# A linear-attention kernel with a token mixer: another written order, constants built with fewer instructions, and the last two output tiles computed in halves

## The chip, the core and the metric

The kernel runs on one core of a Trainium2 chip. The core has a matrix engine (PE in the profile, with its weight loads as PEld), three engines that work on 128 partitions at once (DVE, ACT, POOL), and a queue engine (SP) that here only starts transfers. The metric is the time of one execution on the device in microseconds (us); lower is better.

## The reference

For each of 4 batches and 8 heads, attention with a decay of `lam` per token runs over blocks of 64 tokens of 64 features: inside a block with a masked product, between blocks through a state. The eight heads side by side are then the input `x` of a mixer over tokens.

```python
for b in range(nb):                                   # 12 blocks of 64 tokens
    intra = einsum('bhic,bhjc->bhij', qb, kb) * Dmask[None]     # lam ** (i - j), lower triangle
    intra = einsum('bhij,bhjd->bhid', intra, vb)
    inter = einsum('bhid,bhde->bhie', qb * lam_pow[None], kv_state)
    out[:, :, sl] = intra + inter
    kv_state = lam_block * kv_state + einsum('bhsd,bhse->bhde', kb * rev_pow, vb)
...
x = out as [4, 768, 512]
W_tok = (x @ w_q) @ (x @ w_k).T / 8                   # [768, 768] per batch
result = maximum(W_tok @ x, 0) @ w_out                # [4, 768, 512], float32
```

## The kernel before

The kernel works on 16 pairs of heads, n = 0 to 15, four pairs to a batch, and on chunks of 128 tokens, six to a sequence. Decay is taken out of the blocks: q is multiplied by lam^t (the tiles `dq`) and v by lam^-t (the tile `DvI`), so that the mask is a plain triangle. The operands of the matrix engine are bf16, sums are f32.

All instructions are issued in an order written out by hand, the string `ORDER`. A word is a piece, its index, the PSUM bank it uses (`@`), and the engine that does it (`:a` ACT, `:v` DVE, `:p` POOL). Each engine takes its own instructions in that order, and waits where an operand or a bank is not ready. The pieces:

- `q`, `k`, `v`, `wq`, `wk`, `wo`: loads with a cast from f32 to bf16, all issued on POOL's queue (lines 113, 117, 121, 127, 132, 140). Eight semaphores take turns, so that a load is issued only when the one eight places earlier has landed.
- `sv`: v times `DvI`, in place, on DVE or POOL (line 239).
- `Aq`, `Ak`: transposes of q and k on PE (251, 260); `eq`, `ek`: their copies out of PSUM, `eq` with the factor `dq` (266, 234).
- `S0`, `S1`: scores of the first and the last three chunks (277). `M0`, `M1`: DVE multiplies them with the mask on the way out of PSUM (291). `Mc` and `Mm` do this in two steps: ACT copies the scores out (306), DVE multiplies in place (310). This form exists for the first half only.
- `P`: states, the running sums of k times v (319). For n below `WHOLE` = 6 every chunk adds to all later ones; from there on the first two chunks add to two places only, and `G` (copy of the states, 328) adds the missing part on DVE in three instructions (335 to 337).
- `I`, `V`: the two products that make the attention output (347, 359); `ex`: its copy to `xnat`. `F`, `ef`: its transpose with the permutation `order` (382) and the copy to `xT`.
- `Q` (in parts `Qp`), `K`, `Y`, `m` with their copies: the mixer's products for a batch (404, 414, 430, 455, 479, 490). `O`, `eo`: a 128x512 output tile, its copy out of PSUM and its store on SP's queue (508, 519). Twelve tiles `osb` hold outputs.
- `Z`: matmuls of zeros (528), 512 columns each, which keep PE at work; nine stand at the start.
- `hold`: a small transfer on SP's queue that waits for k of pair 14, so that no store starts earlier.

Tokens are permuted inside a chunk: q is loaded in pairs of rows, and `order` brings the attention output to the same sequence. `ident` and `order` are built on DVE from a ramp `ET` and the partition number `row` (lines 157 to 203); `blank` is the tile of zeros.

Of the kernel before, what the change touches and what calls it, by code (L numbers as in the profile page):

```python
# [9 lines left out]
BF16 = mybir.dt.bfloat16  # L10
F32 = mybir.dt.float32
ALU = mybir.AluOpType
ACT = mybir.ActivationFunctionType

B, H, S, D = 4, 8, 768, 64
CH = 128
NCH = S // CH
HD = H * D
DHY = 64
NP = H // 2  # L20
HALF = 3 * CH
N = B * NP
WHOLE = 6
R = (slice(0, 64), slice(64, 128))
# [5 lines left out]
q.2 k.2 v.2 q.3 k.3 v.3 wq.0 wk.0 q.4 k.4 v.4 wo.0 q.5 k.5 v.5 q.6 k.6 v.6 q.7 k.7 v.7 sv.4:p q.8  # L30
k.8 v.8 sv.5:p q.9 k.9 v.9 q.10 k.10 v.10 sv.7:p q.11 k.11 v.11 q.12 k.12 v.12 sv.9:p q.13 k.13
v.13 sv.10:p q.14 k.14 v.14 sv.11:p q.15 k.15 v.15 sv.12:p sv.13:p sv.14:p hold.14 Aq.0@0 dq.2
eq.0@0 dq.3 Z.5@7 Ak.0@0 dq.1 ek.0@0:v Z.3@7 S1.0@0 sv.0:v S0.0@2 Mc.0@2 M1.0@0 Z.3@7 P.0@4 Aq.1@5
G.0@4:a Mm.0:v Z.1@7 I.0@0 eq.1@5 Ak.1@4 V.0@0 ek.1@4:v ex.0@0:a S0.1@4 sv.1:v S1.1@2 Mc.1@4 Z.1@7
F.0@0 M1.1@2 P.1@1 ef.0@0:a Aq.2@4 Mm.1:v G.1@1:a eq.2@4 Z.1@7 Ak.2@0 I.1@2 ek.2@0:v V.1@2 S1.2@0
sv.2:v ex.1@2:a S0.2@4 Mc.2@4 M1.2@0 Z.3@7 P.2@2 Aq.3@3 G.2@2:a Mm.2:v F.1@4 eq.3@3 Ak.3@2
ef.1@4:v I.2@0 V.2@0 ek.3@2:v ex.2@0:a sv.3:v Z.1@7 S0.3@2 S1.3@4 cw.0:a M1.3@4 Mc.3@2 Z.2@7 P.3@0
Qp.0.0@1 F.2@6 G.3@0:a Mm.3:v Qp.0.1@1 ef.2@6:a I.3@4 V.3@4 Qp.1.0@0 ex.3@4:a Aq.4@6 Ak.4@7 eq.4@6
F.3@4 ek.4@7:a Qp.1.1@0 Qp.0.2@1 eg.3.0@4:v Qp.1.2@0 eg.3.1@4:v Qp.0.3@1 eQ.0.0@1:v Qp.1.3@0
S1.4@4 eQ.0.1@0:a Kh.0.0@1 M1.4@4 ek2.0.0@1:a Kh.0.1@0 S0.4@6 ek2.0.1@0:a M0.4@6 Y.0@0 YA.0@0:a  # L40
YB.0@0:v Aq.5@1 YC.0@0:a m.0.1@6@7 eq.5@1 m.0.0@4@5 eh.0.1.0@6:a eh.0.0.0@4:v eh.0.0.1@5:a Ak.5@1
eh.0.1.1@7:a m.0.2@4@6 ek.5@1:v m.0.3@5@0 eh.0.2.1@6:a eh.0.3.1@0:v S0.5@2 eh.0.3.0@5:a S1.5@6
eh.0.2.0@4:v P.4@0 O.0.5@5 G.4@0:v M1.5@6 I.4@0 eo.0.5@5:a V.4@0 M0.5@2 Aq.6@4 ex.4@0:a Ak.6@5
eq.6@4 O.0.4@6 ek.6@5:a sv.6:v S1.6@4 S0.6@0 M1.6@4 F.4@7 O.0.3@2 ef.4@7:a M0.6@0 P.5@3 eo.0.3@2:a
Ak.7@7 G.5@3:v Aq.7@0 ek.7@7:a P.6@2 eq.7@0 I.5@4 V.5@4 G.6@2:v S0.7@0 ex.5@4:a eo.0.4@6:v Aq.8@7
M0.7@0 I.6@2 S1.7@4 O.0.0@6 eq.8@7 M1.7@4 V.6@2 eo.0.0@6:a O.0.2@7 ex.6@2:a sv.8:v P.7@6
eo.0.2@7:a Ak.8@2 G.7@6:v P.8@3 ek.8@2:a F.5@7 G.8@3:v Aq.9@6 ef.5@7:a Ak.9@2 eq.9@6 S1.8@4
ek.9@2:a S0.8@0 I.7@6 M1.8@4 V.7@6 F.6@2 ex.7@6:a M0.8@0 O.0.1@3 ef.6@2:v F.7@6 eo.0.1@3:a Aq.10@7
ef.7@6:v S0.9@2 eq.10@7 S1.9@0 Ak.10@6 M1.9@0 Q.1.0@7 ek.10@6:a M0.9@2 Q.1.1@4 eQ.1.0@7:a I.8@6
eQ.1.1@4:a S1.10@0 P.9@5 M1.10@0 K.1@4 V.8@6 eK.1@4:a G.9@5:v Aq.11@2 ex.8@6:a Y.1@4 eq.11@2  # L50
Ak.11@5 YA.1@4:a YB.1@4:v S0.10@2 ek.11@5:v YC.1@4:a m.1.0@6 M0.10@2 em.1.0@6:a m.1.1@0 Aq.12@5
P.10@4 em.1.1@0:a eq.12@5 m.1.3@2 I.9@6 G.10@4:v em.1.3@2:a V.9@6 m.1.2@0 ex.9@6:v I.10@4
em.1.2@0:a F.8@2 V.10@4 ef.8@2:v S0.11@0 ex.10@4:a S1.11@6 M0.11@0 O.1.1@2 M1.11@6 F.9@3
eo.1.1@2:a O.1.0@0 ef.9@3:a Ak.12@2 eo.1.0@0:a P.11@3 ek.12@2:v Ak.13@1 Aq.13@0 G.11@3:v ek.13@1:a
S1.12@6 S0.12@4 eq.13@0 I.11@2 V.11@2 M0.12@4 O.1.4@0 ex.11@2:a M1.12@6 F.10@1 eo.1.4@0:a F.11@2
ef.10@1:a S0.13@6 ef.11@2:v S1.13@4 Ak.14@0 M1.13@4 P.13@1 ek.14@0:a Aq.14@2 G.13@1:v Q.2.0@3
eq.14@2 Q.2.1@0 eQ.2.0@3:a M0.13@6 S1.14@2 eQ.2.1@0:a I.13@4 O.1.5@1 M1.14@2 V.13@4 sv.15:v
eo.1.5@1:a P.14@0 ex.13@4:a Aq.15@2 G.14@0:v K.2@1 Ak.15@3 eK.2@1:a P.12@4 eq.15@2 P.15@0
ek.15@3:a Y.2@1 G.12@4:v G.15@0:v S0.14@4 YB.2@1:a S0.15@2 I.12@6 YA.2@1:a M0.14@4 V.12@6 YC.2@1:a
O.1.2@0 ex.12@6:a M0.15@2 S1.15@4 eo.1.2@0:a I.14@6 m.2.1@2 M1.15@4 F.12@1 em.2.1@2:a V.14@6  # L60
ef.12@1:a I.15@4 ex.14@6:v m.2.2@2 V.15@4 em.2.2@2:a F.13@0 ex.15@4:v F.14@1 ef.13@0:a m.2.0@2
m.2.3@6 ef.14@1:v F.15@4 em.2.0@2:a O.1.3@0 ef.15@4:v em.2.3@6:a Q.3.0@1 eo.1.3@0:a Q.3.1@6
eQ.3.0@1:a O.2.0@0 eQ.3.1@6:v K.3@1 eo.2.0@0:v O.2.4@6 eK.3@1:a Y.3@7 eo.2.4@6:a O.2.3@6 YA.3@7:v
YB.3@7:v YC.3@7:v m.3.1@0 eo.2.3@6:a O.2.2@4 em.3.1@0:a m.3.0@6 eo.2.2@4:a m.3.2@2 m.3.3@0
em.3.0@6:v O.2.5@5 em.3.2@2:a em.3.3@0:a O.2.1@4 eo.2.5@5:v O.3.0@0 eo.2.1@4:a O.3.2@1 eo.3.0@0:v
O.3.4@4 eo.3.2@1:a O.3.3@5 eo.3.4@4:v O.3.1@1 eo.3.3@5:a O.3.5@0 eo.3.1@1:a eo.3.5@0:a
# [4 lines left out]
def kernel(  # L71
# [11 lines left out]
    nc = tc.nc  # L83
    mm = nc.tensor.matmul
# [54 lines left out]
    def load_wo(_):  # L139
# [17 lines left out]
    blank = consts.tile([128, HD], BF16, name="blank")  # L157
# [3 lines left out]
    nc.vector.memset(step[:, 0:1], 1.0)  # L161
    nc.vector.memset(step[:, 64:65], -125.0)
    one = consts.tile([128, 1], F32, name="one")
    nc.vector.memset(one, 1.0)

    ET = consts.tile([128, S], F32, name="ET")
    nc.vector.tensor_tensor_scan(
        out=ET[:, 0:CH], data0=step, data1=step, initial=0.0, op0=ALU.add, op1=ALU.bypass
# [17 lines left out]
    token = consts.tile([128, 1], F32, name="token")  # L186
    nc.vector.tensor_tensor(out=token, in0=row, in1=row, op=ALU.add)
    for r in range(2):
        nc.vector.tensor_tensor(
            out=token[R[r], :], in0=token[R[r], :],  # L190
            in1=ET[R[r], (0, CH - 1)[r] : (1, CH)[r]], op=ALU.subtract,
        )

    order = consts.tile([128, 128], BF16, name="order")
    nc.vector.tensor_tensor(
        out=order.rearrange("e (p r) -> e p r", r=2), in0=natural,
        in1=token.unsqueeze(2).to_broadcast([128, 64, 2]), op=ALU.is_equal,
    )
    nc.vector.tensor_tensor(out=row, in0=row, in1=one, op=ALU.subtract)
    E6 = consts.tile([128, NCH], F32, name="E6")  # L200
    nc.vector.tensor_tensor(
        out=E6, in0=ET[:, ::CH], in1=row.to_broadcast([128, NCH]), op=ALU.add
# [10 lines left out]
    def make_dq(kk):  # L213
        nc.scalar.activation(out=Dq[kk], in_=ET, func=ACT.Exp, scale=lncol[:, kk : kk + 1])
# [18 lines left out]
    def copy(eng, to, of):  # L233
        return (nc.scalar.copy if eng == "a" else nc.vector.tensor_copy)(out=to, in_=of)  # L234
# [65 lines left out]
    def whole(n):  # L300
        return n < WHOLE


    def drawn(n, o):
        pr[n, 0] = tsb.tile([128, 2, HALF], BF16, tag="pr0", name="pr")
        nc.scalar.copy(out=pr[n, 0], in_=PS[:, o : o + 2, 0:HALF])

    def masked_late(n, eng):
        of = pr[n, 0].rearrange("j l (c i) -> j l c i", c=3)
        (nc.gpsimd if eng == "p" else nc.vector).tensor_tensor(  # L310
            out=of, in0=of, in1=mask2, op=ALU.mult
        )

    def states(n, o):
        to = PS[:, o, 0 : (NCH - 1) * D].rearrange("e (c f) -> e c f", c=NCH - 1)
        for c in range(NCH - 1):
            end = 2 if c < 2 and not whole(n) else NCH - 1
            for hl in range(2):
                mm(  # L319
                    to[R[hl], c:end, :],  # L320
                    fk[n][:, hl, c, :],
                    vn[n][:, hl, c, :].unsqueeze(1).to_broadcast([128, end - c, D]),
                    start=(c == 0),
                    stop=(c == NCH - 2),
                    skip_group_check=True,
                )

    def summed(n, o, eng):
        gs[n] = tsb.tile([128, NCH - 1, D], BF16, tag="gs", name="gs")
        of = PS[:, o, 0 : (NCH - 1) * D].rearrange("e (c f) -> e c f", c=NCH - 1)  # L330
        if whole(n):
            copy(eng, gs[n], of)
            return
        two = small.tile([128, 1, D], F32, tag="two", name="two")
        nc.vector.tensor_copy(out=two, in_=of[:, 1:2, :])
        nc.vector.tensor_copy(out=gs[n][:, 0:2, :], in_=of[:, 0:2, :])
        nc.vector.tensor_tensor(
            out=gs[n][:, 2:, :],
            in0=of[:, 2:, :],
            in1=two.to_broadcast([128, NCH - 3, D]),  # L340
            op=ALU.add,
        )
# [177 lines left out]

    held = consts.tile([1, D], BF16, name="held")
# [3 lines left out]

    def zeros(count, o):
        for _ in range(count):
            mm(PS[:, o, :], blank[:, 0:128], blank, start=True, stop=True)  # L528

    zeros(WARM, 7)  # L530
    make_dq(0)
    make_dv(0)
    pieces = dict(
        q=load_q, k=load_k, v=load_v, wq=load_wq, wk=load_wk, cw=copy_wq, wo=load_wo, hold=hold, dq=make_dq, dv=make_dv,
        sv=scale_v, Aq=turn_q, Ak=turn_k, eq=turned_q, ek=turned_k, S0=scores(0), S1=scores(1),
        M0=masked(0), M1=masked(1), Mc=drawn, Mm=masked_late, P=states, G=summed, I=inter, V=values, ex=attended, F=flip,
        ef=flipped, eg=flipped_half, Q=mix_q, eQ=mixed_q, K=mix_k, eK=mixed_k, Kh=mix_k_half, ek2=mixed_k_half, Y=mix_y, YA=mixed_y, YB=crossed_y(0), YC=crossed_y(1), Qp=mix_q_part, m=mix_m,
        em=mixed_m, eh=mixed_m_half, O=mix_o, eo=mixed_o, Z=zeros,
# [37 lines left out]
```

## Time and profile before

| | us |
|---|---|
| five runs | 98.55, 98.88, 99.70, 99.88, 99.95; median 99.7 |
| the profiled execution | 99.93 |
| its span, first to last instruction | 98.2 |
| mean granted clock | 0.995 |

Where the engines spend the span, in 40 slices of 2.46 us (a digit is the busy share in tenths):

```profile
PE   5999898599988999999799899999999999999930
DVE  5738892994789999998798599699999845544200
ACT  5576385258649367478457496776589992493440
POOL 5999996799669999999999999980000000000000
DMA  0999999999999999999999999999950202545782
```

The costliest group of each engine (instructions, busy time, mean of one; then idle time before them and who ended it):

```profile
L291 DVE TENSOR_TENSOR pr<-ps,mask 128x768 bf16<-128x768 f32 x28 | 25.9, 950 | 0.8 <-PE ps L277 0.7
L508 PE MATMUL ps<-wo,rmT 128*128 128x512 bf16 x86 | 22.7, 380 | 0.6 <-issue 0.2
L117 POOL DMA_DIRECT2D fk<-in_k_dram x16 | 16.7, 1047 | 1.5 <-DMA wo<-in_moe_w_out_dram 1.3
L234 ACT COPY osb<-ps 128x512 f32<-128x512 f32 x19 | 11.2, 588 | 10.0 <-PE ps L508 8.9
L239 POOL TENSOR_TENSOR fv<-fv,DvI 128x768 bf16<-128x768 bf16 x9 | 13.4, 1511 | 0.0
```

Line 234 is a helper's: all plain copies stand there, told apart by their tiles. A POOL instruction of a load is the making of its descriptors; the transfer itself follows and takes several us to land. Matmuls are pipelined, so the mean of one (380 ns for 512 columns) is longer than their spacing (32 of them take 7.03 us at the end, 0.22 each).

### The profile page before, as it was taken

To read this page: it belongs to the slowest core of one execution; us is meant where nothing else is said; L and a number is where in the kernel's file an instruction comes from. 1 tells how busy PE (TensorE), PEld (TensorE's weight loads), DVE (VectorE), ACT (ScalarE), POOL (GpSimd) and SP (SyncE) were. 2 spreads that over 40 slices of the span, in tenths; PEclk is the share of its full clock that TensorE was granted. 3 is DMA by queue.
4 is the path that set the end of the run, shared out by engine and by line. 5 is a ranking of instruction groups with operands and counts; after the bars stand their busy time and mean duration, and the time that the engine had idled before them with its cause. 6 is when DMAs were issued, how large, how long until landed. Compare 5 with 4: busy or idle time off the path is not lost.

```text
span 98.2 us, 3411 instructions
## 1 busy us (share of the span) xinstructions
PE 88.0 (90%) x1455; PEld 56.4 (57%) x1469; DVE 72.0 (73%) x140; ACT 61.5 (63%) x101; POOL 61.5 (63%) x65
## 2 busy tenths in 40 slices
PE   5999898599988999999799899999999999999930
PEld 1345675467564666767566586777696754534400
DVE  5738892994789999998798599699999845544200
ACT  5576385258649367478457496776589992493440
POOL 5999996799669999999999999980000000000000
PEclk9999999999999999999999999999999999999997
DMA  0999999999999999999999999999950202545782
GB/s 1 97 144 154 163 158 168 158 163 192 184 166 160 166 162 165 165 162 165 168 162 164 166 165 160 168 212 393 391 210 9 107 7 107 214 156 216 285 309 102
DMA packets 67438, 16.60 MB, mean 169 GB/s; under 512 B 63840, under 2 KB 64352, under 8 KB 67424
## 3 DMA queue, kind: packets, MB, share of 16 engines
q0 software_dynamic: 63792, 10.10, 139.3%
q1 hardware_dynamic: 3632, 6.30, 17.0%
q8 instruction: 11, 0.18, 0.7%
q14 instruction: 3, 0.02, 0.1%
HBM read 20.19 MB, written 6.29 MB: 270 GB/s over the span
## 4 chain that ended last, share of the span: by engine, by line
PE 66%; DMA 8%; POOL 8%; DVE 7%; issue 4%; ACT 3%; POOLq 0%; ACTq 0%
PE ps L508 21%; DMA fv<-in_v_dram 8%; PE ps L359 6%; PE ps L277 6%; PE ps L382 5%; PE ps L260 5%; PE ps L319 4%; PE ps L404 4%; PE ps L251 4%; PE ps L455 3%; POOL fk L117 3%; PE ps L347 3%; POOL fq L113 3%; PE ps L479 2%; POOL fv L121 2%
## 5 line engine op out<-in xcount | busy, mean ns | idle before, releaser
L291 DVE TENSOR_TENSOR pr<-ps,mask 128x768 bf16<-128x768 f32 x28 | 25.9, 950 | 0.8 <-PE ps L277 0.7
L508 PE MATMUL ps<-wo,rmT 128*128 128x512 bf16 x86 | 22.7, 380 | 0.6 <-issue 0.2
L117 POOL DMA_DIRECT2D fk<-in_k_dram x16 | 16.7, 1047 | 1.5 <-DMA wo<-in_moe_w_out_dram 1.3
L121 POOL DMA_DIRECT2D fv<-in_v_dram x16 | 16.7, 1042 | 1.6 <-DMA fv<-in_v_dram 1.2
L234 ACT COPY osb<-ps 128x512 f32<-128x512 f32 x19 | 11.2, 588 | 10.0 <-PE ps L508 8.9
L113 POOL DMA_DIRECT2D fq<-in_q_dram x16 | 14.1, 882 | 1.1 <-POOLq L560 0.8
L234 ACT CAST xnat<-ps 128x768 bf16<-128x768 f32 x13 | 10.4, 799 | 6.6 <-PE ps L359 6.3
L239 POOL TENSOR_TENSOR fv<-fv,DvI 128x768 bf16<-128x768 bf16 x9 | 13.4, 1511 | 0.0
L508 PEld LDWEIGHTS <-rmT 128*128 128x128 bf16 x96 | 8.3, 98 | 8.6 <-issue 0.7
L490 ACT ACTIVATE rmT<-ps 128x768 bf16<-128x768 f32 (+1 forms) x16 | 10.6, 722 | 0.2
L266 DVE TENSOR_TENSOR qT<-ps,dq 128x768 bf16<-128x768 bf16 x16 | 8.8, 553 | 2.2 <-PE ps L251 2.0
L528 PE MATMUL ps<-blank 128*128 128x512 bf16 x25 | 8.6, 471 | 1.5 <-DVE blank L158 1.2
L277 PE MATMUL ps<-qT,kT 64*128 64x128 bf16 x192 | 9.0, 218 | 0.6 <-DVE kT L234 0.5
L234 ACT COPY kT<-ps 128x768 bf16<-128x768 bf16 x9 | 7.2, 799 | 2.9 <-PE ps L260 2.4
L319 PE MATMUL ps<-fv,fk 128*64 128x128 bf16 (+4 forms) x160 | 7.8, 229 | 1.3 <-DVE fv L239 1.3
L359 PE MATMUL ps<-fv,pr 128*128 128x64 bf16 x192 | 8.5, 194 | 0.5 <-issue 0.5
L239 DVE TENSOR_TENSOR fv<-fv,DvI 128x768 bf16<-128x768 bf16 x7 | 7.1, 1010 | 2.0 <-DMA fv<-in_v_dram 2.0
L260 PE MATMUL ps<-ident,fk 128*64 128x128 bf16 x192 | 8.3, 221 | 0.2
L251 PE MATMUL ps<-ident,fq 128*64 128x128 bf16 x192 | 8.3, 221 | 0.1
L319 PEld LDWEIGHTS <-fk 128*64 128x64 bf16 x160 | 6.0, 110 | 4.0 <-DVE fv L239 2.2
L382 PE MATMUL ps<-order,xnat 128*128 128x128 bf16 x96 | 7.8, 220 | 0.2 <-ACT xnat L234 0.2
L277 PEld LDWEIGHTS <-kT 64*128 64x128 bf16 x192 | 5.6, 94 | 4.1 <-DVE kT L234 1.5
(68 smaller groups left out, 130.2 us busy)
## 6 DMA issues: line engine op xcount, KB each, us to landing
out_dram<-osb SPq DMA_DIRECT2D x24, 256.0 KB, 2.0
fq<-in_q_dram POOLq DMA_DIRECT2D x16, 192.0 KB, 7.6
fk<-in_k_dram POOLq DMA_DIRECT2D x16, 192.0 KB, 8.1
fv<-in_v_dram POOLq DMA_DIRECT2D x16, 192.0 KB, 8.1
wo<-in_moe_w_out_dram POOLq DMA_DIRECT2D x1, 512.0 KB, 8.7
wqk<-in_moe_w_q_dram POOLq DMA_DIRECT2D x1, 64.0 KB, 7.8
wqk<-in_moe_w_k_dram POOLq DMA_DIRECT2D x1, 64.0 KB, 7.5
lam_all<-in_lam_dram SPq DMA_DIRECT2D x1, 4.0 KB, 2.5
```

The lines of the kernel that those rows point to most:

```text
L113: nc.gpsimd.dma_start(out=fq[n], in_=rows_q(n))
L117: nc.gpsimd.dma_start(out=fk[n], in_=rows(n, k))
L121: nc.gpsimd.dma_start(out=fv[n], in_=rows(n, v))
L234: return (nc.scalar.copy if eng == "a" else nc.vector.tensor_copy)(out=to, in_=of)
L239: (nc.gpsimd if eng == "p" else nc.vector).tensor_tensor(out=vn[n], in0=fv[n], in1=DvI[:, 2 * kk : 2 * kk + 2, :].unsqueeze(3).to_broadcas ...
L260: nc.tensor.transpose(PSH[R[hl], o, c * CH : (c + 1) * CH], fk[n][:, hl, c, :], ident)
L277: mm(PS[:, o + hl, cc * CH : (cc + 1) * CH], kT[n][R[hl], c], qT[n][R[hl], c], start=True, stop=True, skip_group_check=True,)
L291: nc.vector.tensor_tensor(out=pr[n, a].rearrange("j l (c i) -> j l c i", c=3), in0=PS[:, o : o + 2, 0:HALF].rearrange("j l (c i) -> j l c ...
L319: mm(to[R[hl], c:end, :], fk[n][:, hl, c, :], vn[n][:, hl, c, :].unsqueeze(1).to_broadcast([128, end - c, D]), start=(c == 0), stop=(c == ...
L359: mm(PS[:, o + hl, c * D : (c + 1) * D], pr[n, c // 3][:, hl, (c % 3) * CH : (c % 3 + 1) * CH], vn[n][:, hl, c, :], start=False, stop=(c = ...
L382: nc.tensor.transpose(PSH[:, o, c * CH : (c + 1) * CH], xnat[b][:, c, kk * CH : (kk + 1) * CH], order,)
L508: mm(PS[:, o, :], rmT[b][:, kt].rearrange("f n i -> f (n i)")[:, t * CH : (t + 1) * CH], wo[:, kt, :], start=(kt == 0), stop=(kt == 3),)
```

## The change

1. The constants on DVE: `one`, `token` and two small memsets go; the scan starts at -1. Zeros and ramp share a tile, so that `blank` is now a 128x128 f32 tile. A permutation `back` is one comparison, PE transposes it, and ACT copies the result to `order`.
2. `Z` multiplies f32 zeros: one matmul stands for up to four of the units before (512 columns for four, 128 for one). The order holds 26 units, and 20 before, beside the nine at the start.
3. `Mc` and `Mm` take either half of a pair: eleven such halves instead of four, and 21 `M` instead of 28.
4. Whole or halved states are chosen by the word (`Pw` with `G`, `P` with `Gp`): whole for pairs 0 to 4, 6 and 7, and 0 to 5 before.
5. Tiles 0 and 5 of the last batch are computed in halves of 256 columns (`Oh`, `oh`); each is stored whole after its second half.
6. The order is another throughout: the loads, the scalings on POOL (eleven and not nine), the copies between ACT and DVE, and the sequence on PE.

```diff
 ORDER = """
-q.2 k.2 v.2 q.3 k.3 v.3 wq.0 wk.0 q.4 k.4 v.4 wo.0 q.5 k.5 v.5 q.6 k.6 v.6 q.7 k.7 v.7 sv.4:p q.8
-k.8 v.8 sv.5:p q.9 k.9 v.9 q.10 k.10 v.10 sv.7:p q.11 k.11 v.11 q.12 k.12 v.12 sv.9:p q.13 k.13
-v.13 sv.10:p q.14 k.14 v.14 sv.11:p q.15 k.15 v.15 sv.12:p sv.13:p sv.14:p hold.14 Aq.0@0 dq.2
+q.2 k.2 v.2 q.3 k.3 v.3 wq.0 wk.0 q.4 k.4 v.4 q.5 k.5 v.5 q.6 k.6 v.6 q.7 sv.4:p k.7 v.7 sv.5:p
+q.8 k.8 v.8 wo.0 sv.6:p q.9 sv.7:p k.9 v.9 q.10 k.10 v.10 q.11 k.11 v.11 q.12 sv.9:p k.12 v.12
+q.13 sv.10:p k.13 v.13 sv.11:p q.14 k.14 sv.12:p v.14 q.15 k.15 sv.13:p v.15 sv.14:p sv.15:p
...
+Mc.0.7@0 M1.7@6 S0.6@2 Pw.6@5 Mm.0.7:v Pw.7@4 G.6@5:a M0.6@2 F.5@6 G.7@4:a ef.5@6:a I.7@4 I.6@0
+V.6@0 sv.8:v V.7@4 ex.6@0:a Aq.8@6 Ak.8@7 ex.7@4:a eq.8@6 P.8@0 ek.8@7:v F.6@1 F.7@6 Gp.8@0
...
-O.3.4@4 eo.3.2@1:a O.3.3@5 eo.3.4@4:v O.3.1@1 eo.3.3@5:a O.3.5@0 eo.3.1@1:a eo.3.5@0:a
+oh.3.5.1@6:a O.3.2@0 eo.3.4@1:v O.3.3@6 eo.3.2@0:v O.3.1@1 eo.3.3@6:a Oh.3.0.0@0 eo.3.1@1:v Oh.3.0.1@4 oh.3.0.0@0:a
+Oh.3.5.0@6 oh.3.0.1@4:v oh.3.5.0@6:a
 """
...
-    blank = consts.tile([128, HD], BF16, name="blank")
+    ramp = consts.tile([128, CH + S], F32, name="ramp")
+    blank = ramp[:, 0:CH]
+    ET = ramp[:, CH:]
     nc.vector.memset(blank, 0.0)
...
-    token = consts.tile([128, 1], F32, name="token")
-    nc.vector.tensor_tensor(out=token, in0=row, in1=row, op=ALU.add)
-    for r in range(2):
-        nc.vector.tensor_tensor(
-            out=token[R[r], :], in0=token[R[r], :],
-            in1=ET[R[r], (0, CH - 1)[r] : (1, CH)[r]], op=ALU.subtract,
-        )
+    back = consts.tile([128, 128], BF16, name="back")
+    nc.vector.tensor_tensor(
+        out=back, in0=ET[:, 0:CH], in1=row.to_broadcast([128, CH]), op=ALU.is_equal
+    )
...
-    def drawn(n, o):
+    def drawn(a, n, o):
+        pr[n, a] = tsb.tile([128, 2, HALF], BF16, tag=f"pr{a}", name="pr")
+        nc.scalar.copy(out=pr[n, a], in_=PS[:, o : o + 2, 0:HALF])
...
+    def mix_o_half(b, t, half, o):
+        at = slice(half * 256, (half + 1) * 256)
+        for kt in range(4):
+            mm(
+                PS[:, o, 0:256],
+                rmT[b][:, kt].rearrange("f n i -> f (n i)")[:, t * CH : (t + 1) * CH],
+                wo[:, kt, at],
+                start=(kt == 0),
+                stop=(kt == 3),
+            )
...
+    def mixed_o_half(b, t, half, o, eng):
+        at = slice(half * 256, (half + 1) * 256)
+        whole = (b, t) in part
+        if not whole:
+            part[b, t] = outp.tile([128, HD], F32, tag="osb", name="osb")
+        copy(eng, part[b, t][:, at], PS[:, o, 0:256])
+        if whole:
+            nc.sync.dma_start(out=out[b, t * CH : (t + 1) * CH, :], in_=part[b, t])
...
     def zeros(count, o):
-        for _ in range(count):
-            mm(PS[:, o, :], blank[:, 0:128], blank, start=True, stop=True)
+        while count > 0:
+            n = min(count, 4) * CH
+            mm(PS[:, o, 0:n], blank, blank[:, 0:1].to_broadcast([128, n]), start=True, stop=True)
+            count -= 4
 
     zeros(WARM, 7)
+    nc.tensor.transpose(PSH[:, 6, 0:CH], back, ident)
     make_dq(0)
     make_dv(0)
+    nc.scalar.copy(out=order, in_=PSH[:, 6, 0:CH])
```

## The prediction, made before the changed kernel ran

> **What bounds the kernel now.** I read the engine shares first, then the stretches, then the queue of loads on POOL, then the chain that ended last.
>
> ```profile
> PE 88.0 (90%) x1455; PEld 56.4 (57%) x1469; DVE 72.0 (73%) x140; ACT 61.5 (63%) x101; POOL 61.5 (63%) x65
> ...
> 0.00:22.00 22.00, 18.50 (x279) 10.77 (x283) 16.15 (x38) 12.30 (x21) 19.28 (x26) 1.00 1.85 134
> 22.00:37.70 15.70, 14.81 (x241) 9.43 (x242) 12.91 (x21) 10.14 (x19) 14.00 (x15) 1.00 2.09 172
> 37.70:67.00 29.30, 27.81 (x593) 20.69 (x598) 25.09 (x50) 19.88 (x31) 28.20 (x26) 1.00 2.22 174
> 67.00:94.20 27.20, 26.84 (x354) 15.52 (x352) 17.85 (x34) 18.62 (x31) 0.00 (x0) 1.00 0.50 190
> 94.20:98.20 4.00, 0.00 (x0) 0.00 (x0) 0.00 (x0) 0.58 (x1) 0.00 (x0) 0.87 0.47 176
> ```
>
> The columns of the stretches are length, busy time of PE, PEld, DVE, ACT and POOL, then the granted clock, DMA share and GB/s. TensorE sets the pace: it idles 3.5 us before 22, 0.9 us from 22 to 37.7, 1.5 us from 37.7 to 67, 0.4 us from 67 to 94.2. In the third stretch DVE is at 86% and POOL at 96%, so PE's idle time there is owed to others. In the fourth it is owed to nobody; the last 4.0 us are one copy, one store and the close.
>
> ```profile
> 17.53 1.01 POOL L121 DMA_DIRECT2D fv<-in_v_dram  x1 [1.19 <-DMA fv<-in_v_dram]
> 18.53 0.77 POOL L140 DMA_DIRECT2D wo<-in_moe_w_out_dram  x1
> ...
> 27.55 1.02 POOL L117 DMA_DIRECT2D fk<-in_k_dram  x1 [1.32 <-DMA wo<-in_moe_w_out_dram]
> 28.93 1.01 POOL L121 DMA_DIRECT2D fv<-in_v_dram  x1 [0.36 <-issue]
> 29.95 1.48 POOL L239 TENSOR_TENSOR fv<-fv,DvI 128x768 bf16<-128x768 bf16 x1
> 31.37 0.89 POOL L113 DMA_DIRECT2D fq<-in_q_dram  x1
> ```
>
> POOL issues every load (q about 0.85 us apart, k and v 1.0, wo 0.8) and some of the v scalings (1.42 apart). Each load waits for the one eight places earlier: the two DMA releasers above are that. From 30 on POOL never waits: its own instruction list is what spaces the loads.
>
> **The pieces, priced.** PE pieces by the chain's narrowest figures, us: Aq and Ak 0.34, S 0.25, whole P 0.53, halved P 0.26, I 0.15, V 0.35, F 0.34, Q 1.30, Qp 0.16, K 0.20, Y 0.66, m 0.33, O 0.87. Summing the written order between P.3 (21.99 in the trace), P.5 (37.73), P.13 (66.97) and the last O (94.17) gives 12.7, 26.6 and 29.0 of pieces in 15.7, 29.3 and 27.2 of time: paces of 1.24, 1.10 and 0.94. These paces, not the busy shares, say what a stretch would give.
>
> **Constants and the permutation.** Gone from DVE: memsets of 0.06 twice and 0.11 (0.27 to 0.17), token 0.15 + 2 x 0.15, row 0.15; back replaces order at 0.29. That is 0.84 us, and DvI (done at 5.66) comes about 0.3 earlier. Nobody gains: q.0 lands at 5.11, and scaling v.0 waits for its DMA until 8.38. Added: one transpose on PE behind ident, and a 128x128 copy on ACT between DvI and dq.1, bounded by 0.24 (DvI, 48 columns) and 0.48 (qk, 384); I take 0.3. dq.1 to dq.3 end at 8.14 now; the first use of dq.1 is at 10.59, and order's first flip at 12.81. Zero, with over 2 us of cover on each; without cover 0.3.
>
> **Fillers.** The order holds 26 units instead of 20, beside the same 9 at the start, all ahead of P.3; a unit warm is 0.21 us. They become f32, up to four units in one matmul, with no f32 matmul in this trace: one such costs at least a bf16 unit, 0.21, and at most four of 0.38 (the unpipelined O row), 1.5; I take 4 x 0.21, what it replaces. Six more are 1.3 us of PE in a stretch where PE idles 3.5, and the gate below leaves more room. Zero; 1.3 uncovered, up to 2 at the dearer price.
>
> The Trainium skill (FP8 and Floating Point Precision, TensorE Precision Notes) gives true FP32 four passes through the array, which no run here shows. By it the price is the one taken, and the sum does not move.
>
> **Loads and scalings: the new gate.** wo goes from behind v.4 to behind v.8, so q.5 to v.8 are issued earlier and the 1.32 wait on wo goes. But POOL takes on two more scalings (11, not 9) and takes them earlier: in the order sv.4 to sv.7 now stand ahead of k.9. From the end of v.4's issue at 18.53, POOL must pass five q, eight k or v, wo and four scalings before sv.7 is done: 5 x 0.85 + 8 x 1.0 + 0.8 + 4 x 1.42 = 18.7, plus 0.2 of waiting for k.3: 37.5. The order puts Pw.7 directly behind Pw.6, so PE stops there until 37.5 at the earliest. What is queued behind Pw.7 on PE is everything: F.5, I.7, I.6, all later pieces. Up to there PE has 12.6 us of pieces from P.3 in 15.5 (the same as before up to P.5), DVE 15.1 instead of 13.3. Behind Pw.7 stand 27.5 + 28.5 = 56.0 us of pieces; behind P.5 at 37.73 there were 26.6 + 29.0 = 55.6. So at 37.5 the two kernels stand level within 0.3 us, whatever the head saved.
>
> The other end of the queue: from 37.5 to v.15's issue 13 x 1.0 + 6 x 0.85 + 5 x 1.42 = 25.2, so 62.7 where it was 60.5. The last v took 6.6 us to land; then 69.3, and its scaling ends on POOL at 70.8. P.15 is wanted at 71.1 (below). Zero; with the 8.1 us of the median landing it is 1.2 late.
>
> **From the gate to the end.** Up to P.13 DVE has 26.9 us of pieces instead of 28.2: masks drop from 13 to 10, and copies of osb partly return (4, not 1). PE's own 27.5 lie between a pace of 1.047 (its busy time, 27.81 over 26.6: no idle left) and 1.10 (as now). The idle I expect gone sits where DVE was late: PE stands 0.46 at 46.8 ahead of V.8, and around 56 the chain runs through YB, kT and pr on DVE. So 1.047: 28.8 us, P.13 at 66.3; as now it would be 30.3. After P.13 28.5 at 0.94 are 26.7: the last matmul at 93.0, and P.15 (5.2 of pieces after P.13) at 71.1.
>
> **A rule that speaks against it.** DVE multiplying two SBUF operands beside POOL's scaling shows in this trace once:
>
> ```profile
> 34.28 1.50 POOL L239 TENSOR_TENSOR fv<-fv,DvI 128x768 bf16<-128x768 bf16 x1
> ...
> 35.26 1.35 DVE L239 TENSOR_TENSOR fv<-fv,DvI 128x768 bf16<-128x768 bf16 x1
> ```
>
> The median of that DVE form is 0.96: 0.4 us lost. The change has eleven late masks (Mm, also two SBUF operands, 0.55 each) instead of four, at least four of them while POOL scales, and eleven POOL scalings. A collision costs between nothing and 1.5; with the row's 0.4 twice, DVE loses 0.8, of which I put 0.2 on PE's path at DVE's 86%.
>
> The Trainium skill (SBUF — State Buffer, Who interferes with whom) says that such a DVE instruction and a GpSimd one that reads SBUF exclude each other, the later waiting for the whole of the earlier. The row agrees in kind (0.4 lost for an overlap of 0.5). By the rule four collisions could take up to 4 x 1.5 = 6 us of DVE instead of 0.8.
>
> **The tail.**
>
> ```profile
> 93.37 0.58 ACT L234 COPY osb<-ps 128x512 f32<-128x512 f32 x1 [0.28 <-PE ps L508]
> 94.23 0.58 ACT L234 COPY osb<-ps 128x512 f32<-128x512 f32 x1 [0.28 <-PE ps L508]
> ```
>
> A copy of 256 columns takes 0.37 (ACT YA row): 0.21 less after the last matmul. The store stays whole, but tile 3.0's now goes out about 0.4 ahead of it, not 0.86; a 256 KB store at the 309 GB/s of the late slices occupies 0.85, so up to 0.45 comes back. Sixteen matmuls of 256 columns for eight of 512 add 0 to 0.3. Net -0.2 to +0.5; I take 0.
>
> **The sum.** Last matmul 93.0 + 0.2 against 94.17: -1.0. The profiled execution took 99.93 (span 98.2 and 1.73 around it), 0.23 over the median of 99.7. 93.2 + 4.0 + 1.73 - 0.23 = 98.7.
>
> **Rivals.** First, no change: PE keeps the pace of 1.10 after the gate, since PSUM banks and chains are only dealt out anew. For it: the sums are level at 37.5. Then P.13 is at 67.9, the end 94.6: 99.9 to 100.1 with the collisions. Against: DVE's load there falls by 1.3 us. Chance 0.25, reaching 99.2 if half the idle goes.
>
> Second, slower, through POOL: any wait W on a landing between v.4 and sv.7 comes through whole, since PE stands at Pw.7. Before, POOL waited 0.28 + 1.32 + 0.36 = 2.0 there. For it: the eight-deep window is unchanged and landings took up to 10.2 us. Against: the longest wait was wo's, which is moved, and scalings now fill the time. W = 1.0 takes the gain away; 2.0 makes 100.7. Collisions and a late v.15 push the same way. Chance 0.17.
>
> Third, more than forecast: PE after the gate at its bare 27.5, without collisions: P.13 at 65.0, end 91.7, 97.2. Chance 0.08. The forecast has 0.5, its own range 97.4 to 99.4 (bare pace halfway to pace 1.08). That the halved last tiles do not shorten the tail is inside it.
>
> A measurement of this kernel tells about 1% from no change: the five runs span 98.55 to 99.95. Faster than 98.7: 0.7 of the forecast, a tenth of the first rival, all of the third: 0.45. Slower than 100.7: most of the second and a little of the rest: 0.18. Within: 0.37. The range leaves out the third's far end and the worst of the second: 97.2 to 100.6.
>
> **What will show it.** PE idle ahead of a P line near 36 to 37.6, released by POOL's scaling, and that scaling ending at 37.5: the gate. v.15 issued near 62.7, and P.15 not waiting. PE busy over 98% between 37.5 and 66, DVE's late masks near 0.55, the last matmul at 93.2, 4.0 us behind it. I am wrong if PE runs through Pw.7 without a stop, if the masks are stretched to 1 us and more, if PE still idles 1.5 us in the third stretch, or if fillers move P.3 beyond 25.

## The result, and the profile after

The changed kernel takes 100.36 us (median of 48 runs, 99.32 to 102.3) where the kernel before takes 99.63 (88 runs on the same chips, 98.55 to 101.44). The ratio of the times is 1.007, 95% interval 1.0053 to 1.0086: within 1%, but on the slower side, and 1.66 us above the forecast of 98.7. Medians here are over all executions, while ratios leave out those more than 1.5% above the fastest of their kernel, so the two can differ. The profiled execution took 99.85, its span 97.9; so it lies 0.5 under the median, which will matter.

The page of the changed kernel: busy time of each engine, PE and POOL in 40 slices, the chain that ended last by engine, and POOL's scalings.

```profile
PE 88.7 (91%) x1466; PEld 58.4 (60%) x1475; DVE 74.2 (76%) x140; ACT 61.7 (63%) x101; POOL 64.7 (66%) x67
...
PE   5999999999998789999999999999699999999930
...
POOL 5999999599999999999999999970500000000000
...
POOL 57%; PE 22%; DMA 8%; issue 6%; POOLq 2%; ACT 1%; DVE 0%; DVEq 0%
...
L229 POOL TENSOR_TENSOR fv<-fv,DvI 128x768 bf16<-128x768 bf16 x11 | 16.7, 1519 | 4.0 <-DMA fv<-in_v_dram 4.0
```

PE has one new hollow, the 6 at the 29th slice (69 to 71 us). POOL is empty one slice ahead of it and busy for half a slice beside it, and the group of its scalings waited 4.0 us, all of it for one v to land. The chain of waits now runs through POOL for 57% of the span; before, it ran through PE for 66%:

```profile
PE 66%; DMA 8%; POOL 8%; DVE 7%; issue 4%; ACT 3%; POOLq 0%; ACTq 0%
```

The stretches of the changed kernel (length, then busy time of PE, PEld, DVE, ACT, POOL, granted clock, DMA share, GB/s):

```profile
...
22.00:37.60 15.60, 13.95 (x293) 9.88 (x293) 13.23 (x27) 10.88 (x21) 15.57 (x16) 1.00 2.26 165
37.60:67.00 29.40, 28.54 (x569) 20.43 (x575) 26.20 (x50) 20.19 (x31) 27.93 (x27) 1.00 2.10 175
67.00:71.10 4.10, 3.11 (x64) 2.17 (x66) 3.24 (x8) 3.38 (x6) 1.47 (x1) 1.00 1.25 356
71.10:93.80 22.70, 22.48 (x265) 12.91 (x267) 16.24 (x28) 12.69 (x23) 0.00 (x0) 1.00 0.42 163
93.80:97.90 4.10, 0.01 (x1) 0.00 (x0) 0.03 (x1) 0.37 (x1) 0.00 (x0) 0.91 0.52 197
```

In 37.6 to 67 PE is idle for 0.86 us, where it was 1.5 before. The loss stands in the short stretch behind: 1.0 us of 4.1. The timeline there (start, length, engine, line, work, and in brackets the wait ahead of it), POOL first, then SP, then PE:

```profile
36.11 1.49 POOL L229 TENSOR_TENSOR fv<-fv,DvI 128x768 bf16<-128x768 bf16 x1
...
62.96 1.08 POOL L122 DMA_DIRECT2D fv<-in_v_dram  x1
64.06 1.49 POOL L229 TENSOR_TENSOR fv<-fv,DvI 128x768 bf16<-128x768 bf16 x1
69.53 1.47 POOL L229 TENSOR_TENSOR fv<-fv,DvI 128x768 bf16<-128x768 bf16 x1 [3.99 <-DMA fv<-in_v_dram]
...
62.36 0.59 SPq L543 DMA_DIRECT2D held<-fk  x1
62.99 7.50 SPq L515 DMA_DIRECT2D out_dram<-osb  x9
...
37.90 1.02 PE L311 MATMUL ps<-fv,fk 128*64 128x320 bf16 x20
...
65.87 0.45 PE L311 MATMUL ps<-fv,fk 128*64 128x128 bf16 x10
...
71.06 0.42 PE L311 MATMUL ps<-fv,fk 128*64 128x128 bf16 x9 [0.89 <-POOL fv L229]
```

POOL's lines are sv.7 (done at 37.60), the load of v.15, sv.14, and sv.15 after 3.99 us of waiting for v.15. At the moment when v.15 is issued (62.96), SP starts on the stores that `hold` had kept back (62.99): eight tiles lay ready, and nine stores are issued by 70.5. PE's lines are Pw.6 with Pw.7, P.13, and P.15, which waits 0.89 us for sv.15. In the kernel before, v.15 was issued 2.6 us ahead of the first store:

```profile
60.52 1.04 POOL L121 DMA_DIRECT2D fv<-in_v_dram  x1
...
63.09 13.08 SPq L519 DMA_DIRECT2D out_dram<-osb  x11
```

It landed 6.6 us after its issue, at 67.1, and DVE took it at 70.47: some 3 us of cover that the changed order does not have.

### The profile page after: what moved, and what is told of

It reads as the page before. It is cut to its first block, busy times and chain, and to the rows that moved or that the text cites. A ratio compares the mean times of both kernels' runs of the same rounds, so it can differ in the third digit from the quotient of the medians.

```text
span 97.9 us, 3428 instructions
## 1 busy us (share of the span) xinstructions
PE 88.7 (91%) x1466; PEld 58.4 (60%) x1475; DVE 74.2 (76%) x140; ACT 61.7 (63%) x101; POOL 64.7 (66%) x67
## 4 chain that ended last, share of the span: by engine, by line
POOL 57%; PE 22%; DMA 8%; issue 6%; POOLq 2%; ACT 1%; DVE 0%; DVEq 0%
POOL fv L229 15%; POOL fk L118 14%; POOL fv L122 14%; POOL fq L114 12%; PE ps L504 10%; DMA fk<-in_k_dram 8%; PE ps L521 2%; PE ps L475 2%; PE ps L355 2%; POOLq L595 2%; PE ps L451 2%; PE ps L378 1%; PE ps L400 1%; PE ps L343 1%; POOL wo L141 1%
## 5 line engine op out<-in xcount | busy, mean ns | idle before, releaser
L504 PE MATMUL ps<-wo,rmT 128*128 128x512 bf16 x79 | 20.7, 380 | 0.7 <-issue 0.3
L281 DVE TENSOR_TENSOR pr<-ps,mask 128x768 bf16<-128x768 f32 x21 | 19.7, 952 | 2.0 <-PE ps L267 2.0
L229 POOL TENSOR_TENSOR fv<-fv,DvI 128x768 bf16<-128x768 bf16 x11 | 16.7, 1519 | 4.0 <-DMA fv<-in_v_dram 4.0
L549 PE MATMUL ps<-ramp 128*128 128x512 f32 (+3 forms) x26 | 11.7, 563 | 1.1 <-DVE ramp L162 1.1
L224 DVE COPY osb<-ps 128x512 f32<-128x512 f32 (+1 forms) x13 | 8.7, 671 | 4.9 <-PE ps L504 3.6
L224 ACT COPY osb<-ps 128x512 f32<-128x512 f32 (+1 forms) x13 | 7.0, 537 | 6.9 <-PE ps L504 3.9
L293 ACT CAST pr<-ps 128x768 bf16<-128x768 f32 x11 | 8.8, 806 | 2.8 <-PE ps L267 2.8
L224 ACT COPY kT<-ps 128x768 bf16<-128x768 bf16 x10 | 8.0, 809 | 3.2 <-PE ps L250 1.7
L224 ACT COPY xT<-ps 128x768 bf16<-128x768 bf16 (+1 forms) x10 | 7.7, 770 | 1.9 <-PE ps L378 1.8
L486 ACT ACTIVATE rmT<-ps 128x768 bf16<-128x768 f32 (+1 forms) x12 | 8.0, 683 | 0.6 <-PE ps L475 0.5
```

The lines of the kernel that those rows point to most:

```text
L229: (nc.gpsimd if eng == "p" else nc.vector).tensor_tensor(out=vn[n], in0=fv[n], in1=DvI[:, 2 * kk : 2 * kk + 2, :].unsqueeze(3).to_broadcas ...
L281: nc.vector.tensor_tensor(out=pr[n, a].rearrange("j l (c i) -> j l c i", c=3), in0=PS[:, o : o + 2, 0:HALF].rearrange("j l (c i) -> j l c ...
L293: nc.scalar.copy(out=pr[n, a], in_=PS[:, o : o + 2, 0:HALF])
L504: mm(PS[:, o, :], rmT[b][:, kt].rearrange("f n i -> f (n i)")[:, t * CH : (t + 1) * CH], wo[:, kt, :], start=(kt == 0), stop=(kt == 3),)
L549: mm(PS[:, o, 0:n], blank, blank[:, 0:1].to_broadcast([128, n]), start=True, stop=True)
```

## The experiments

Theory A: the longer list on POOL issues v.15 later, and its landing and its scaling on POOL now end what PE waits for at P.15; A1: the landing is long because the stores that `hold` releases move beside it. A rival to A1 is A2: it is long from the loads' own queue, whatever the stores do. Rivals to A: the later POOL list costs nothing by itself, and the loss is that of the halved last tiles, of the f32 fillers (D1), or of PE waiting at Pw.7 for sv.7. The times of the kernel before that stand beside each experiment come from the same chips. "Outside" is the time of an execution less its span, as a mean over the executions of a kernel.

**v.15 issued one scaling earlier.**

```diff
-q.15 k.15 sv.13:p v.15 sv.14:p sv.15:p
+q.15 k.15 v.15 sv.13:p sv.14:p sv.15:p
```

> One edit of the changed kernel: on POOL's list v.15 is issued before the scaling of pair 13, not behind it. Theory A (the list of POOL is what sets the end: last load v.15, its landing, its scaling on POOL, then P.15): v.15 is issued about 1.4 us earlier, P.15 no longer waits 0.9 us, and the median falls by 0.8 to 1.4 us against the changed kernel (100.4 to about 99.3), with less spread from run to run. Theory B (the loss sits in the tail: halves, buffers, stores): no change beyond 0.2 us. Theory C (collisions of DVE and POOL): no change beyond 0.2 us.

Measured: 98.98 us (12 runs), ratio 0.9939 (0.9913 to 0.9966). Its timeline, POOL and then PE:

```profile
61.63 1.04 POOL L121 DMA_DIRECT2D fv<-in_v_dram  x1
...
68.67 1.47 POOL L228 TENSOR_TENSOR fv<-fv,DvI 128x768 bf16<-128x768 bf16 x1 [3.08 <-DMA fv<-in_v_dram]
...
70.20 0.42 PE L310 MATMUL ps<-fv,fk 128*64 128x128 bf16 x9 [0.15 <-POOL fv L228]
```

Issued 1.33 earlier, v.15 is scaled 0.86 earlier, and P.15 starts 0.86 earlier: one for one. The median fell by 1.38, more than that, since the profiled execution of the changed kernel is one of its better ones. One swap of two words turns 0.7% slower into 0.6% faster, so A holds, and the rest of the change is a gain.

**One more multiplication on POOL.** A spare product into a tile that nobody reads, behind v.14.

```diff
-sv.12:p v.14 q.15 k.15 sv.13:p v.15
+sv.12:p v.14 idle.0 q.15 k.15 sv.13:p v.15
...
+    def idle(_):
+        nc.gpsimd.tensor_tensor(
+            out=spare, in0=fv[12],
+            in1=DvI[:, 0:2, :].unsqueeze(3).to_broadcast([128, 2, NCH, D]), op=ALU.mult,
+        )
```

> One more multiplication of 1.4 us on POOL, into a spare tile that nobody reads, behind v.14's load, so that v.15 is issued 1.4 us later. Theory A: every microsecond of POOL comes through: 1.2 to 1.5 us slower than the changed kernel, about 101.7. Theory B: hidden, at most 0.2 us slower. Theory C: hidden but for a collision, at most 0.5 us.

Measured: 105.56 us (6 runs, 103.49 to 107.0), ratio 1.0454 (1.0397 to 1.0511), far more than the 1.2 to 1.5 us expected. The profiled execution took 106.53. Timeline (SP, POOL, PE) and the clock in 40 slices:

```profile
63.45 9.28 SPq L514 DMA_DIRECT2D out_dram<-osb  x10
...
65.36 1.07 POOL L121 DMA_DIRECT2D fv<-in_v_dram  x1
...
74.13 1.47 POOL L228 TENSOR_TENSOR fv<-fv,DvI 128x768 bf16<-128x768 bf16 x1 [6.19 <-DMA fv<-in_v_dram]
...
75.65 0.69 PE L310 MATMUL ps<-fv,fk 128*64 128x128 bf16 x10 [4.86 <-POOL fv L228]
```

```profile
PEclk9999999999999999999999999999655999999999
```

One more scaling (1.4 us) delays P.15 by 4.6 here. The issue is 2.4 later, 1.9 us behind the first store now, and the landing takes another 2.2. From P.15 to the end of the span pass 28.95 us (104.6 less 75.65) where the changed kernel takes 26.84: 2.1 more, at the place where the granted clock falls behind PE's long wait. So A holds, with two amplifiers that the expectation did not have: the stores, and the clock.

**The last two tiles whole.**

```diff
-O.2.0@0 eo.2.5@1:v Oh.3.5.1@6 eo.2.0@0:v O.3.4@1 oh.3.5.1@6:a O.3.2@0
+O.2.0@0 eo.2.5@1:v eo.2.0@0:v O.3.4@1 O.3.2@0
...
-Oh.3.0.0@0 eo.3.1@1:v Oh.3.0.1@4 oh.3.0.0@0:a Oh.3.5.0@6 oh.3.0.1@4:v oh.3.5.0@6:a
+O.3.0@0 eo.3.1@1:v O.3.5@6 eo.3.0@0:v eo.3.5@6:a
```

> The changed kernel with the last two tiles computed and copied whole, as before, tile 5 last. Theory B (the halves cost in the tail): 0.3 to 0.7 us faster than the changed kernel, part of it perhaps outside the span, where the changed kernel has 1.93 us and the one before 1.73. Theory A: the tail is worth what the copy row says, 0.2 us slower to 0.2 us faster.

Measured: 100.79 us (6 runs), ratio 1.0107 (1.0072 to 1.0141), which overlaps that of the changed kernel; by the medians alone it stays unclear. The profile tells more:

```profile
71.67 0.42 PE L309 MATMUL ps<-fv,fk 128*64 128x128 bf16 x9 [1.36 <-POOL fv L227]
```

P.15 starts 0.61 later here, and the span is 98.5 instead of 97.9: from P.15 to the end 26.83 us whole, 26.84 in halves. In these two executions the halves bring nothing and cost nothing.

**bf16 fillers, from a tile of their own.**

```diff
+    zero = consts.tile([128, HD], BF16, name="zero")
+    nc.vector.memset(zero, 0.0)
...
-        while count > 0:
-            n = min(count, 4) * CH
-            mm(PS[:, o, 0:n], blank, blank[:, 0:1].to_broadcast([128, n]), start=True, stop=True)
-            count -= 4
+        for _ in range(count):
+            mm(PS[:, o, :], zero[:, 0:128], zero, start=True, stop=True)
```

> The changed kernel with bf16 matmuls of zeros, one for each unit, in the same places. All theories: within 0.2 us, since everything ahead of 22 us is covered by POOL's list. A rival D (the f32 fillers delay the head, or carry the 0.2 us outside the span): 0.2 to 0.5 us faster.

Measured: 100.96 us (7 runs), ratio 1.0099 (1.0052 to 1.0146): the fillers are not the cause of the loss. In its profiled execution (102.59 us, one of the longer of the seven) v.15, issued at 63.02, is scaled at 70.97, and P.15 waits 2.38. So with the issue within 0.2 us of the same place the lag was 6.6 us in one execution, 7.0 in another (the whole tiles) and 8.0 in this one. The clock in 40 slices:

```profile
PEclk9999999999999999999999999999966999999999
```

It falls behind this wait too, and from P.15 to the end (72.50 to 100.8) pass 28.3 us, 1.5 more than the 26.84 of the changed kernel. The time outside the span fell from 1.94 to 1.77.

**The stores released one k later, and one k earlier.** `hold` waits for k of pair 15, or of pair 13; POOL's list is untouched.

```diff
-hold.14
+hold.15
```

> The changed kernel, with the stores held back until k of pair 15 has landed, not k of pair 14. Theory A with A1 (v.15 lands late because the held stores, freed at k.14 near 62.4, share the transfer engines with it): v.15 issued near 63 lands after about 5 us, not 6.6 to 8, P.15 waits little, and the median falls by 0.7 to 1.3 us against the changed kernel, to about 99.3. Theory A with A2 (the landing is late from the loads' own eight-deep queue): landing unchanged at 6.5 us or more, no change beyond 0.2 us. Theory B (tail): stores that start later end later, 0 to 0.5 us slower.

```diff
-hold.14
+hold.13
```

> The changed kernel, with the stores freed earlier, when k of pair 13 has landed (about 58). A1: nine stores of 256 KB compete with the loads of pairs 14 and 15 as well; v.15 lands later still or P.13 and P.15 wait, 0.5 to 2 us slower than the changed kernel. A2: no change beyond 0.2 us; or, if the burst is over before v.15 is issued, faster.

Measured: released later, 99.21 us (12 runs), ratio 0.9949 (0.9911 to 0.9988). Released earlier, 107.16 (6 runs, 105.02 to 109.66, too scattered for an interval). Timelines, released later and then released earlier:

```profile
66.62 10.02 SPq L514 DMA_DIRECT2D out_dram<-osb  x11
...
62.85 1.08 POOL L121 DMA_DIRECT2D fv<-in_v_dram  x1
...
67.33 1.47 POOL L228 TENSOR_TENSOR fv<-fv,DvI 128x768 bf16<-128x768 bf16 x1 [1.89 <-DMA fv<-in_v_dram]
```

```profile
59.77 9.22 SPq L514 DMA_DIRECT2D out_dram<-osb  x10
...
62.97 1.08 POOL L121 DMA_DIRECT2D fv<-in_v_dram  x1
...
74.55 1.47 POOL L228 TENSOR_TENSOR fv<-fv,DvI 128x768 bf16<-128x768 bf16 x1 [8.93 <-DMA fv<-in_v_dram]
...
76.08 0.69 PE L310 MATMUL ps<-fv,fk 128*64 128x128 bf16 x10 [5.41 <-POOL fv L228]
```

The same load, issued within 0.12 us of the same moment, is scaled 4.5, 6.6 or 11.6 us later as the first store goes out at 66.62, 62.99 or 59.77. That is A1; A2 alone would have left the landing as it was. The loss with the early release is far beyond the 0.5 to 2 us expected: the best of the six executions took 105.02, the profiled one 107.08. (The profiled execution released later lost time at other places, 100.71 us against its median of 99.21; only these rows are read from it. The version further down with sv.7 earlier, released later too, gives the same lag in an execution of 99.14:)

```profile
66.78 12.35 SPq L514 DMA_DIRECT2D out_dram<-osb  x12
...
63.30 1.08 POOL L121 DMA_DIRECT2D fv<-in_v_dram  x1
...
67.62 1.47 POOL L228 TENSOR_TENSOR fv<-fv,DvI 128x768 bf16<-128x768 bf16 x1 [1.74 <-DMA fv<-in_v_dram]
```

**Both remedies together.**

```diff
-q.15 k.15 sv.13:p v.15 sv.14:p sv.15:p hold.14
+q.15 k.15 v.15 sv.13:p sv.14:p sv.15:p hold.15
```

> v.15 issued ahead of the scaling of pair 13, and stores held until k.15. A1: v.15 issued near 61.6 lands near 66.6, the gate at P.15 is gone altogether, P.15 at 70.1: 0.1 to 0.4 us faster than with the earlier issue alone (98.98), with a smaller spread. A2: the same as the earlier issue alone.

Measured: 99.36 us (12 runs), ratio 0.9962 (0.9922 to 1.0002), and P.15 at 69.93 without a wait. With the wait gone either way, the second remedy adds nothing that 12 runs show; the 0.1 to 0.4 us expected did not come.

**The control: the kernel before, with its stores released later.**

```diff
-sv.12:p sv.13:p sv.14:p hold.14
+sv.12:p sv.13:p sv.14:p hold.15
```

> Control: the kernel before, with the stores held until k.15. There v.15 is issued at 60.5, lands near 67.1 and is scaled at 70.5, so 3 us lie between. All theories: within 0.2 us of the kernel before (99.6).

Measured: 99.42 us (12 runs), ratio 1.0004 (0.9968 to 1.0040). The later release is no gain in itself; it gains only where v.15 has no cover. The trace holds one thing more: the issue of v.15, the first store, and the time from that issue to the landing:

```profile
60.90 1.04 POOL L120 DMA_DIRECT2D fv<-in_v_dram  x1
...
66.84 9.02 SPq L518 DMA_DIRECT2D out_dram<-osb  x11
...
fv<-in_v_dram POOLq DMA_DIRECT2D x1, 192.0 KB, 6.6
```

With the first store 5.9 us behind it the load takes 6.6 us, as it did with the store 2.6 us behind it. In the kernel before, moving the stores does not move its landing.

**Stores later, and bf16 fillers.** The fillers are those of the experiment above.

```diff
-hold.14
+hold.15
...
+            mm(PS[:, o, :], zero[:, 0:128], zero, start=True, stop=True)
```

> Stores held until k of pair 15, and bf16 fillers in the places of the f32 ones. In the runs so far the time outside the span was 1.93 us with f32 fillers and 1.78 with bf16 ones. Theory D1 (f32 fillers cost time outside the span): 1.75 to 1.80 outside, median 0.15 us below 99.21, near 99.05, the span as there. Theory D2 (chance, or another part of the change): 1.93 outside, the same median.

Measured: 98.71 us (12 runs), ratio 0.9925 (0.9897 to 0.9953), the lowest median of this study, ahead of both kernels; its interval overlaps those of the other remedies. Outside the span lie 1.78 us.

**f32 fillers in the kernel before.**

```diff
-    blank = consts.tile([128, HD], BF16, name="blank")
+    blank = consts.tile([128, CH], F32, name="blank")
...
-        for _ in range(count):
-            mm(PS[:, o, :], blank[:, 0:128], blank, start=True, stop=True)
+        while count > 0:
+            n = min(count, 4) * CH
+            mm(PS[:, o, 0:n], blank, blank[:, 0:1].to_broadcast([128, n]), start=True, stop=True)
+            count -= 4
```

> The kernel before with the f32 fillers alone, in its own order. D1: 1.90 to 1.95 us outside the span instead of 1.75, the span unchanged, the median 0.1 to 0.25 us above the kernel before. D2: no change, 1.75 outside. If f32 fillers delay the head more than the waits there cover, the span grows by up to 1 us.

Measured: 99.62 us (12 runs), ratio 1.0002 (0.9967 to 1.0038); outside the span 1.77. So f32 fillers as such cost nothing that 12 runs show, neither inside nor outside: D1 falls.

**sv.7 earlier (with the stores released later).**

```diff
-sv.6:p q.9 sv.7:p k.9 v.9
+sv.6:p sv.7:p q.9 k.9 v.9
...
-hold.14
+hold.15
```

> Stores held until k of pair 15, and the scaling of pair 7 moved ahead of q.9's load on POOL, so that it ends 0.85 us earlier, near 36.8. Theory G (the scaling of pair 7 is a second gate, level with TensorE's own work): PE's states of pairs 6 and 7 start up to 0.8 us earlier only if PE is there by then; 0 to 0.4 us faster than 99.21. If PE was not held by it at all: no change beyond 0.2 us, and those states start near 37.8 as before.

Measured: 99.31 us (12 runs), ratio 0.9957 (0.9925 to 0.9989), against 99.21 with the late stores alone: no gain. POOL, then PE:

```profile
34.00 3.07 POOL L228 TENSOR_TENSOR fv<-fv,DvI 128x768 bf16<-128x768 bf16 x2
...
38.02 1.02 PE L310 MATMUL ps<-fv,fk 128*64 128x320 bf16 x20
```

sv.7 is done at 37.07 instead of 37.60, and PE comes to Pw.6 at 38.02 instead of 37.90. PE is not held there by POOL.

**f32 zeros in a tile of their own (with both remedies).**

```diff
+    zero = consts.tile([128, CH], F32, name="zero")
+    nc.vector.memset(zero, 0.0)
...
-            mm(PS[:, o, 0:n], blank, blank[:, 0:1].to_broadcast([128, n]), start=True, stop=True)
+            mm(PS[:, o, 0:n], zero, zero[:, 0:1].to_broadcast([128, n]), start=True, stop=True)
```

> v.15 ahead of the scaling of pair 13, stores held until k of pair 15, and the f32 zeros in a tile of their own instead of the ramp's. If the time outside the span comes from the fillers sharing the ramp's tile: 1.78 us outside and a median near 98.9. If it belongs to f32 fillers in this order: 1.93 us, as in the run with the first two edits alone, and a median near 99.2. The span should stay near 97.0 either way.

Measured: 99.02 us (12 runs), ratio 0.9945 (0.9915 to 0.9976); outside the span 1.78, where the same kernel with the zeros in the ramp's tile has 1.93.

## Why the prediction was wrong

The forecast of faster failed; the rival that named a late v.15 among its causes had the right side, and its main mechanism, a wait ahead of Pw.7, was not the one. Nearest in number was the first rival, no change (99.9 to 100.1), but by luck: PE's pace behind the gate did improve, and the loss at P.15 came on top. The miss of 1.66 us falls into four parts. For the profiled execution the sum had 98.93 (93.2 + 4.0 + 1.73), and 99.85 came: the last matmul 0.6 late (93.8), the tail 0.1 longer, 0.2 more outside the span. The other 0.74 is that the profiled execution was 0.23 above the median before and is 0.51 below it now.

- **v.15: the step that failed.** "The last v took 6.6 us to land; then 69.3, and its scaling ends on POOL at 70.8. P.15 is wanted at 71.1 (below). Zero". The issue (62.96 for 62.7) and the landing in the profiled execution (6.6) came as written, and sv.15 ended at 71.0. Two things were wrong. PE was ready at 70.17, not 71.1: P.13 came 0.4 earlier, and the pieces behind it, 5.2 us that at the pace of 0.94 were put at 4.9, took 4.3. A cover of 0.3 was thus none, and every further gain of PE's would have gone into the same wait. In the profiled execution P.15 thus stood where the sum had it (71.06 for 71.1), and the wait took 0.9 us that PE had gained beyond the forecast. And the 6.6 was the landing of another load: one issued 1.0 us behind k.15 and 2.6 us ahead of the stores, which takes 6.6 with later stores too. The new one is issued 2.45 us behind k.15, and takes 4.3 to 4.5 us where the stores start more than 3 us behind it; but the stores were not moved with it, so that it starts beside them and takes 6.6 or more. That the profiled execution shows 6.6 again is luck. Its landing then varies (lags of 6.6, 7.0 and 8.0 in three profiled executions of nearly the same order, with the issue within 0.2 us of the same place), and each of the three pays the difference at P.15, with a lower clock on top where the wait was longest. That this is also the 0.51 between the profiled execution and the median is inferred from those three; the other executions have no profile. The text had the price, "with the 8.1 us of the median landing it is 1.2 late", and put it in a rival instead of in the sum. With the wait gone, or cut to 0.15 us, the kernel takes 98.98 to 99.36, in three ways, so the rest of the sum was off by no more than 0.3 to 0.7.
- **The gate at Pw.7.** Its time was right (sv.7 done at 37.60 for 37.5), its effect not: PE comes to Pw.6 at 37.90 by its own work and shows no wait on POOL, and sv.7 half a microsecond earlier changes nothing. The condition "if PE runs through Pw.7 without a stop" is met. That PE and POOL stood level near 37.5 was a coincidence of two lists.
- **From the gate to P.13.** 28.0 us (37.90 to 65.87) for the forecast 28.8. PE's two longest idle times there before, 0.46 and 0.42 us, are gone, and the longest left is 0.19; here the profiled execution gains. That DVE had caused them is the prediction's reading, which no run shows: the profile puts both down to issue.
- **From P.15 to the last matmul.** 22.74 for 22.1: mis-sized by 0.6, the same in the kernel with v.15 ahead (22.77).
- **Collisions of DVE with POOL.** "At least four" late masks beside a scaling; one was:

```profile
32.82 1.10 DVE L297 TENSOR_TENSOR pr<-pr,mask 128x768 bf16<-128x768 bf16 x1
...
33.61 1.64 POOL L229 TENSOR_TENSOR fv<-fv,DvI 128x768 bf16<-128x768 bf16 x1
```

  The other ten took 0.55 or 0.56, beside no scaling. This one lost 0.55, and PE idled 0.88 behind DVE soon after. The masks mostly missed the scalings, so the trace tests the rule that the prediction feared at one place only, and the mask was late there before the scaling had begun. What stretched it is open.
- **Constants, fillers, tail.** P.3 starts at 22.08 (21.99 before): zero, as put. The order holds 25 units, not the 26 that the text counted, which changes nothing here. Six units of f32 took 1.56 us where five of bf16 had taken 1.25, so 0.26 and 0.25 each: the price that the sum took, one f32 unit for one of bf16. The tail's 4.1 us are the 4.0 of the forecast, and whole tiles gave the same.
- **Outside the span.** 1.94 in the mean, where the sum took 1.73 from the profiled execution before (the mean of the kernel before is 1.78); no step looked there. It goes with the zeros' place in the ramp's tile (1.93 and 1.78 with the tile and its memset as the only difference), not with f32. Why is open.

## What to carry to other kernels

When a change puts work ahead of the last load on a queue, price that load's landing beside whatever else starts to move at that time, and compare it with the time at which the faster kernel wants it, not the old one. A cover smaller than the spread of landings is no cover: the median pays the spread, and one good profiled execution hides it. A step whose end time is predicted well can still hold nobody; only a wait in the trace, or moving it, shows that it gates.

## What the runs showed of the hardware

**Loads beside stores.** The last v of 192 KB, by its issue, the first store's start and the start of its scaling; in the last two rows the lag is that of the load itself, since DVE took it later.

| kernel | v.15 issued | first store | issue to scaling, us |
|---|---|---|---|
| released later | 62.85 | 66.62 | 4.5 |
| released later, sv.7 earlier | 63.30 | 66.78 | 4.3 |
| both remedies | 61.67 | 66.61 | 5.4 |
| v.15 ahead | 61.63 | 62.62 | 7.0 |
| changed kernel | 62.96 | 62.99 | 6.6 |
| one more on POOL | 65.36 | 63.45 | 8.8 |
| released earlier | 62.97 | 59.77 | 11.6 |
| before | 60.52 | 63.09 | 6.6 |
| before, released later | 60.90 | 66.84 | 6.6 |

Read by pairs with the same order of loads: 4.3 to 4.5 becomes 6.6 and 11.6 as the stores start beside the load or 3.2 us ahead of it; 5.4 becomes 7.0 as they start 1.0 us behind it; 6.6 stays as they start 2.6 us behind it. With the stores more than 3 us behind, a v.15 issued 1.0 us behind k.15 takes longer (5.4 and 6.6) than one issued 2.45 us behind it (4.3 and 4.5); what else divides the 5.4 from the 6.6 was not tested.

The Trainium skill (DMA: Bandwidth & Descriptors, Issuing engines are not separate DMA queues) says that transfers started from different engines run on the same sixteen DMA engines and interleave. The table agrees, and puts up to 7 us on it.

**The clock after a wait.** PE's waits at P.15 of 0.9 us (changed kernel) and 1.4 (whole tiles) leave the granted clock at 1.00. The wait of 2.4 (bf16 fillers) is followed by 3.4 us at 0.50, which begin 1.3 us after PE is back; from P.15 to the end the span is 1.5 us longer than in the changed kernel. With the wait of 4.9 (one more product on POOL) the clock is at 0.50 for 6.8 us, the last 4.9 of them behind the wait, and that rest of the span is 2.1 longer. Every execution of the two kernels with a wait near 5 us has a low mean clock: 0.967 to 0.980 with one more product, 0.952 to 0.978 released earlier. With bf16 fillers three of seven have it (0.982 or 0.983, at 102.07 to 102.84 us, the profiled one among them), and four do not (0.992 to 1.00, at 100.14 to 100.96). The Trainium skill (TensorE: Matmul & The Clock Gate, What's actually happening) has the clock halve after an idle window of about 3.4 us. The half clock agrees; but in this one trace a wait of 2.4 us was enough. By these four traces what a late operand costs jumps between 1.4 and 2.4 us of waiting.
